# Linear attention and a routed mixture of experts on one core: a new order of the attention steps, 26 constant matmuls at the head of TensorE's queue, and one DMA for w_phi

## The chip, the cores and the metric

The kernel runs on one core of a Trainium2 chip. The metric is the device time of one execution in microseconds; several runs are summed up by their median. One execution was also profiled. In the profile PE is TensorE's matmuls and PEld its weight loads, DVE is VectorE, ACT is ScalarE, POOL is GpSimd, SP is SyncE; a "q" behind an engine's name means its sequencer, which issues DMAs and waits.

## What is computed

Two stages follow each other. The first is a linear attention (batch 8, 8 heads, 576 tokens, head size 64) with a feature map of 128 exponentials and their reciprocals; the second sends the 4608 tokens of 512 numbers through 8 experts of width 1024, whose results are mixed by a table P that eight rounds of row and column scaling make.

```python
def phi(x):
    proj = np.einsum('bhsd,df->bhsf', x, w_phi)
    proj = proj - np.max(np.abs(proj), axis=-1, keepdims=True)
    return np.concatenate([np.exp(proj), np.exp(-proj)], axis=-1)
q_p, k_p = (phi(q), phi(k))
kv = np.einsum('bhsf,bhsd->bhfd', k_p, v)
z = np.sum(k_p, axis=2)
num = np.einsum('bhsf,bhfd->bhsd', q_p, kv)
den = np.einsum('bhsf,bhf->bhs', q_p, z)[..., None] + 1e-06
# x = num / den, as (4608, 512)
...
P = np.exp(logits)                 # logits = x @ w_gate - max
for _ in range(8):
    P /= P.sum(1, keepdims=True) + 1e-09
    P /= P.sum(0, keepdims=True) + 1e-09
    P *= N / E
for e in range(E):
    out += P[:, e:e + 1] * (np.maximum(x @ w1[e], 0.0) @ w2[e])
```

## The kernel before

**How instructions get their order.** The kernel doesn't issue instructions directly. Each operation is handed to a `Plan` with its engine, an estimated duration, the keys that it reads and writes, and the buffers that it takes. `Plan.schedule` is a list scheduler that runs on the host when the kernel is built: again and again it starts the operation that can start soonest on its engine, and of several that can start at once, the one that was handed in first. What it puts out is the order of each engine's queue. On the chip each engine takes its queue strictly in that order and waits by semaphores, so an estimated duration changes no instruction, but it can change which one stands ahead. The helpers `pe(cols, ...)`, `act(el, ...)`, `dve(el, ...)` and `pool(el, ...)` take a size, from which the duration is worked out; `pe` counts cols/2400 us. `dma(queue, ...)` hands in a transfer with an assumed rate.

**Tiling of the attention.** For each of the 8 batches the first 512 tokens of 4 pairs of heads are worked on as pairs (32 in all), and the last 64 tokens of all heads together as the "rest". The work is cut into steps named by a letter; the string `order` has 322 letters, the n-th occurrence of a letter being that step's n-th piece. Its order is the order in which operations are handed in, and so their priority:

- `l`: loads half a batch of keys, queries and values (`load_qk`, `load_v`). For batches 0 and 1 keys and queries come in fp32 by SP's queue into `acc` tiles that are free then; for batches 2 to 7 in bf16 by POOL's queue into `qk`, and `t` transposes them by a DMA on SP's queue (`turn_qk`, line 550) into `qkT`. `e` loads the rests. A load waits for the maxima of the last `a` and `q` ahead of it.
- `a` (`pair_a`): for batches 0 and 1 first 8 fp32 transposes on TensorE (line 735) of a pair's keys and queries, cast to `qkT` by DVE (line 739) and ACT (line 743); then four token matmuls of the keys by `wphi2` (256 columns each, line 605), two reduces of the absolute maximum on DVE (line 597), four exponentials on ACT (line 601), and the products of the values by the exponentials of the maxima on POOL (line 793).
- `q`: the token matmuls of the queries, two reduces, one small exponential. `p`: two feature-row matmuls (512 columns) and four exponentials. `r` (`rest_a`): all of this for a batch's rest, with 4 fp32 transposes in batches 0 and 1 (line 661).
- `b`, `n`, `m`: the product of keys and values (line 875 copies it), and the two heads' outputs (matmuls of line 888, DVE lines 896 to 902). `c` turns the result into `xT`, on TensorE (line 917) or, in batches 3 to 6, by a DMA transpose. `g`: the rest's turn and the gate.
- `w` loads expert 0's weights. `u` and `d` are quarters of expert 0's first and second layer (`up0`, `down0`); an up step takes 8 matmuls of 512 columns, needs `c` of the batch's four pairs, and appears in the profile as `ps<-xT,w`. These steps fill TensorE's free time.

**Start of the program.** SP's queue issues the first pair's keys, queries and values; ACT's queue issues two DMAs that load the same `w_phi` (64 by 128, fp32) into the lower and the upper 64 partitions of `wphi_f`. DVE clears `wphi2` (a block diagonal of two copies of `w_phi`), casts each half into it (line 1027), clears the two `vrd` tiles (line 1036), and sets `colw`, a 128 by 128 tile of ones that the routing uses much later.

**After the attention.** `routing` makes P on DVE while TensorE works on expert 0, and experts 1 to 7 then run for some 780 us with a scheme of seven products instead of eight (lines 1391 and 1400). None of that is touched.

Of the kernel before, what the change touches and what calls it, by code (L numbers as in the profile page):

```python
# [13 lines left out]
ACT = mybir.ActivationFunctionType  # L14
# [322 lines left out]
def kernel(  # L337
# [11 lines left out]
    nc = tc.nc  # L349
# [26 lines left out]
    colw = const.tile([128, 128], BF16, name="colw")  # L376
# [11 lines left out]
    wphi_f = a_in.tile([128, DF], FP32, name="wphi_f")  # L388
# [3 lines left out]
    vrd = [a_in.tile([128, 2, NP, 2, D1], BF16, name=f"vrd{i}") for i in range(2)]  # L392
# [7 lines left out]
    def pe(cols, fn, r=(), w=(), takes=()):  # L400
        plan.op("PE", max(cols / 2400.0 + 0.0025, 0.031), 0.22, fn, r, w, takes)
# [4 lines left out]
    def dve(el, fn, r=(), w=(), shared=False):  # L406
        plan.op("DVE", el / 960.0 + 0.07, 0.15, fn, r, w, shared=shared)
# [7 lines left out]
    def dma(queue, nbytes, rate, fn, r=(), w=()):  # L415

        speed, unit = LINK.get(rate, (rate, 40))
        if nbytes == 2 << 20:
            speed, unit = 400, 150
        o = plan.op(queue, 0.8 if queue == "POOL" else 0.6, 0.0, fn, r, w, (), nbytes / speed)  # L420
        o.turn, o.unit = rate == 148, unit
# [67 lines left out]
    def new(tag):  # L489
        return R[tag].new()  # L490
# [113 lines left out]
    def mm(out_, lhsT, rhs, start, stop):  # L604
        nc.tensor.matmul(out_, lhsT=lhsT, rhs=rhs, start=start, stop=stop)  # L605
# [45 lines left out]
    def rest_a(b, t):  # L651

        r = {}
        bi = NP * (b - t["b0"])
        rT = new("rT")
        if b >= 2:
            rk = [(t["qk"], h, x) for h in range(2) for x in range(2)]
        if b < 2:
            ptr = new("PP")
            for pr in range(NP):  # L660
                pe(128, lambda pr=pr: nc.tensor.transpose(
                    ptr()[:, pr * 128:pr * 128 + 128],
                    acc[0][:, b, pr * 128:pr * 128 + 128], identf),
                    [("acc", 0, b, h, x) for h in range(2) for x in range(2)] + ["identf"],
                    [ptr, ("acc", 0, b)])
            dve(512, lambda: nc.vector.tensor_copy(
                out=rT().rearrange("p a b -> p (a b)"), in_=ptr()), [ptr], [rT])
        else:
            dma("SP", 1 << 17, 148, lambda: nc.sync.dma_start_transpose(
                out=rT(), in_=t["qk"]()[:, bi:bi + NP].rearrange("p a b c -> p (a b c)")),  # L670
                rk, [rT])
        m = new("m_r")
        r["E"] = [new(f"kr{x}") for x in range(2)]
        r["T"] = [new(f"qr{x}") for x in range(2)]
        r["r"] = new("r_r")
        r["em"] = new("em_r")
        own = r["E"] + r["T"] + [m, r["r"], r["em"]]
        pp = two(RM)
        tokens(pp, lambda c: rT()[:, c, :], NP, [rT], own)
        if TI:  # L680
            mk = [(m, x) for x in range(2)]
            for x in range(2):
                maxes(512, lambda x=x: m()[:, 2 * x], lambda x=x: pp[1][x]().rearrange(
                    "p (c f) -> p c f", c=NP), [pp[0][x * (1 - RM)]], [(m, x)])
            for x, s in ((0, 1.0), (1, -1.0)):
                exp(512, lambda x=x: r["E"][x]().rearrange("p a b -> p (a b)"),
                    lambda: pp[1][1](), s, pp[0][-1:], [(r["E"][x], 0)])
        else:
            mk = [(m, c) for c in range(2 - RM)]
            for c in range(2 - RM):  # L690
                n = NP // 2 * (1 + RM)

                def sc(c=c, n=n):
                    return pp[0][c]().rearrange("p (a b c) -> p a b c", a=n, b=2)

                maxes(256 * n, lambda c=c, n=n: m()[:, 0:3:2, n * c:n * c + n].rearrange(
                    "p b a -> p a b"), sc, [pp[0][c]], [(m, c)])
                for x, s in ((0, 1.0), (1, -1.0)):
                    exp(128 * n, lambda x=x, c=c, n=n: r["E"][x]()[:, n * c:n * c + n],
                        lambda sc=sc: sc()[:, :, 1, :], s, [pp[0][c]], [(r["E"][x], c)])  # L700
        r["Ek"] = [[(r["E"][x], c) for c in range(1 if TI else 2 - RM)] for x in range(2)]
        pt = new("P1")
        pe(512, lambda: mm(pt()[:, 0:512], wphi2[:, 0, :],
                           rT().rearrange("p a b -> p (a b)"), True, True),
           [rT, "wphi2"], [pt])
        for x, s in ((0, 1.0), (1, -1.0)):
            exp(512, lambda x=x: r["T"][x]().rearrange("p a b -> p (a b)"),
                lambda: pt()[:, 0:512], s, [pt], [r["T"][x]])
        exp(10, lambda: r["r"](), lambda: m()[:, 0], -2.0, mk, [r["r"]])
        pool(8, lambda: nc.gpsimd.tensor_scalar_mul(m()[:, 1], m()[:, 2], -1.0), mk, [(m, "neg")])  # L710
        em, vd = r["em"], vrd[b % 2]
        exp(10, lambda: em(), lambda: m()[:, 1:3], 1.0, mk + [(m, "neg")], [em])
        for h in range(2):
            rows = slice(h * 64, h * 64 + 64)
            pool(512, lambda rows=rows, h=h: nc.gpsimd.tensor_tensor(
                out=vd[rows, :, :, h, 0:D],
                in0=t["v"]()[rows, None, bi:bi + NP].to_broadcast([64, 2, NP, D]),
                in1=em()[rows, :, :, None].to_broadcast([64, 2, NP, D]), op=ALU.mult),
                [(t["v"], h), em], [("vrd", b % 2, h)])
            pool(80, lambda rows=rows, h=h: nc.gpsimd.tensor_copy(  # L720
                out=vd[rows, :, :, h, D], in_=em()[rows]),
                [em], [("vrd", b % 2, h, 1)])
        return r

    def pair_a(b, pr, t):
# [3 lines left out]
        if b < 2:  # L729
            g = t["f"]  # L730
            for x in (1, 0):
                ptr = new("PP")
                i = 2 * x + h0 // 2
                for c in range(4):
                    pe(128, lambda c=c, i=i, ptr=ptr: nc.tensor.transpose(  # L735
                        ptr()[:, c * 128:(c + 1) * 128], acc[g][:, i, c * 128:c * 128 + 128],
                        identf), [("acc", g, i), "identf"], [ptr])
                if x:
                    dve(512, lambda x=x, ptr=ptr: nc.vector.tensor_copy(
                        out=t["T"]()[:, x, 2 * h0:2 * h0 + 4, :].rearrange("p a b -> p (a b)"),  # L740
                        in_=ptr()), [ptr], [(t["T"], x, h0 // 2)])
                else:
                    act(512, lambda x=x, ptr=ptr: nc.scalar.copy(
                        out=t["T"]()[:, x, 2 * h0:2 * h0 + 4, :].rearrange("p a b -> p (a b)"),
                        in_=ptr()), [ptr], [(t["T"], x, h0 // 2)])
# [15 lines left out]
        def scores(x, pp):  # L761
# [32 lines left out]
            out=s["v"]()[:, :, :, 0:D],  # L794
# [219 lines left out]
    for b in range(2):  # L1014
        for i in range(2):
            halves[b, i] = new_half(b, i)
    load_qk(0, 0, 2, halves[0, 0])
    dma("ACT", 1 << 15, 100, lambda: nc.scalar.dma_start(out=wphi_f[0:64, :], in_=w_phi),
        w=["wphi_f0"])
    dma("ACT", 1 << 15, 100, lambda: nc.scalar.dma_start(out=wphi_f[64:128, :], in_=w_phi),  # L1020
        w=["wphi_f1"])
    load_v(0, 0, 2, halves[0, 0])
    pool(300, lambda: make_identity(nc, identf), w=["identf"])
    act(128, lambda: nc.scalar.copy(out=ident, in_=identf), ["identf"], ["ident"])
# [8 lines left out]
    load_qk(0, 4, 4, halves[0, 1])  # L1033
    load_v(0, 4, 4, halves[0, 1])
    for i in range(2):
        dve(450, lambda i=i: nc.vector.memset(vrd[i], 0.0),
            w=[("vrd", i, h, *y) for h in range(2) for y in ((), (1,))])
    dve(128, lambda: nc.vector.memset(colw, 1.0), w=["colw"])
    dma("SP", 1 << 14, 50, lambda: nc.sync.dma_start(
        out=wgate_f, in_=moe_w_gate.rearrange("(c p) e -> p c e", p=128)), w=["wgate_f"])  # L1040
    act(32, lambda: nc.scalar.copy(out=wgate, in_=wgate_f), ["wgate_f"], ["wgate"])
# [25 lines left out]
    def stage_r(b):  # L1067
        rs[b] = rest_a(b, rests[b])
# [4 lines left out]
    def stage_g(b):  # L1073
# [9 lines left out]
             "c": lambda j: pair_c(j // 4, j % 4, xbs[j]), "g": stage_g,  # L1083
             "u": lambda i: up0(i // 4, i % 4), "d": lambda i: down0(i // 4, i % 4)}
    order = (
        "lraeaepqbwlqaqawwabwmqlltnrbppnwqbppmrmanbqaqmwwacmpnpbccpwbtcnmqnaqbclupunm"
        "taumquglcapalbcpnqqdcenmucugbblnapmrcqdutabnqpmunpbambccddnqplanmqmducpblttb"
        "augnaqlnrbdcampcadmqeutunqcppmdcaqtdqabpbbmlrqtdnpmuaqualbnagnacctbmqulupran"
        "tdpmtdqcmdnpdabdancpcabbqmpumqbcdgnappqunburqcbugmmnqdcdanumupqbnucmcpnmbddp"
        "bqmpncncubncmmgccg"  # L1090
    )
    for i, n in enumerate(order):
        at[0] = i
# [626 lines left out]
        return {"out": stores, "X1": X1, "Y1": Y1, "Z1": Z1, "X2": X2, "X3": X3, "Z2": Z2, "X4": X4}  # L1720


    ORDER = "X1 x10 w10 x11 X2 x20 y10 x21 Z1 y11 X3 w11 x30 x31 x40 x41 w20 Y1 w21 X4 Z2".split()
    INNER = ("ib1 ia1 ib2 ib3 X1 ia2 ia3 ia5 ia6 ib5 x20 ib6 ia4 x30 ia7 x40 ib4 x21 X2 y10 "
        "ib7 Z1 x31 X3 w20 Z2 y11 w21 x41 Y1 X4").split()
    EARLY = ("w10 x10 X1 w11 y10 x11 x20 Z1 x30 w20 x21 X2 Y1 x31 w21 X3 Z2 X4 x41 y11 x40").split()
    END = "X1 p2 Y1 X2 Z1 p3 X3 Z2 X4 p0 p1".split()
    slots, wait = list(range(6)), []

    def take():  # L1730
# [91 lines left out]
```

## Time and profile before

| | |
|---|---|
| median of 3 runs | 1014.48 us (1013.58 to 1015.42) |
| profiled execution | 1013.5 us, of which the span from first to last instruction is 1011.7 us |
| TensorE busy | 996.5 us (99%), 8195 matmuls |
| VectorE, ScalarE, GpSimd busy | 851.8, 797.0 and 379.7 us |
| read from and written to memory | 92.62 MB and 14.55 MB |

The page first gives busy time by engine, then the span in 40 slices of about 25 us with a digit for the busy tenths, then DMA queues, the chain that ended last, and the costliest groups of instructions. Other views of the same trace give busy time for chosen stretches, instructions in order of time (with `[idle before <-releaser]`, what the engine had waited for), and DMAs with their time from issue to landing. Matmuls are pipelined: the time of one is longer than the distance to the next.

### The profile page before, as it was taken

Reading aid. Unit: us, or ns where it says so; the run is one execution under the profiler, and the core shown is the slowest. Engines: PE = TensorE matmul, PEld = TensorE weight load, DVE = VectorE, ACT = ScalarE, POOL = GpSimd, SP = SyncE. Lnnn points to the kernel's source line nnn. Section 1 sums busy time; section 2 is a strip of 40 time slices with the busy share of each in tenths; the row PEclk is TensorE's granted clock in tenths of the full one; section 3 lists DMA queues with packets and bytes.
Section 4 is the critical chain, followed back from the end, with each engine's and each line's share of the span. In section 5 each row is a group of like instructions: output and inputs, shape, how many; then the busy total and the mean of one; then the engine's idle time right before and its main releaser. Section 6 shows DMA issues by size and latency. Waiting matters only on the chain.

```text
span 1011.7 us, 22473 instructions
## 1 busy us (share of the span) xinstructions
PE 996.5 (99%) x8195; PEld 713.6 (71%) x8232; DVE 851.8 (84%) x1979; ACT 797.0 (79%) x1786; POOL 379.7 (38%) x418
## 2 busy tenths in 40 slices
PE   7899999999999999999999999999999999999998
PEld 5666666644566867787777777787778777787775
DVE  8999989986888988789788988898778978888775
ACT  8999999836888787777777777768776877777774
POOL 5778764400133323342333323332333333433333
PEclk9999999999999999999999999999999999999999
DMA  9999989150114411171116121341126111612443
GB/s 253 198 191 177 166 148 134 38 115 1 48 48 96 114 48 48 48 138 56 48 48 117 48 57 52 73 93 48 48 51 144 48 48 48 110 53 69 154 154 142
DMA packets 115087, 93.94 MB, mean 93 GB/s; under 512 B 54432, under 2 KB 97440, under 8 KB 114976
## 3 DMA queue, kind: packets, MB, share of 16 engines
q1 hardware_dynamic: 83024, 68.46, 26.4%
q0 software_dynamic: 31648, 23.86, 17.0%
q8 instruction: 64, 1.05, 0.5%
q14 instruction: 47, 0.39, 0.1%
q10 hardware_dynamic: 304, 0.20, 0.1%
HBM read 92.62 MB, written 14.55 MB: 106 GB/s over the span
## 4 chain that ended last, share of the span: by engine, by line
PE 93%; ACT 3%; DVE 1%; DMA 1%; issue 1%; DVEq 0%
PE ps L1391 42%; PE ps L1400 25%; PE ps L605 17%; PE ps L1487 7%; PE ps L888 2%; ACT k L601 1%; ACT q L601 1%; DMA xT<-wx 1%; DVE wx L597 0%; PE ps L735 0%; DMA acc<-in_k_dram 0%; ACT wx L601 0%; PE ps L917 0%; ACT kr L601 0%; DVE m L597 0%
## 5 line engine op out<-in xcount | busy, mean ns | idle before, releaser
L1671 POOL TENSOR_TENSOR acc<-acc,hx 128x512 f32<-128x512 f32 x186 | 236.0, 1269 | 555.0 <-ACT hx L1668 287.5
L1391 PEld LDWEIGHTS <-hs 128*128 128x128 bf16 x1984 | 194.1, 98 | 56.2 <-issue 0.4
L1462 DVE CUSTOM_DVE_ANT_0 hs<-ps,U 128x512 bf16<-128x512 f32 x252 | 167.0, 685 | 46.6 <-PE ps L1400 29.0
L1668 ACT ACTIVATE hx<-ps,P 128x256 f32<-128x256 f32 x372 | 161.2, 482 | 45.2 <-PE ps L1391 42.3
L1467 ACT ACTIVATE hs<-ps 128x512 bf16<-128x512 f32 x252 | 151.1, 609 | 52.6 <-PE ps L1400 45.8
L1656 DVE SCALAR_TENSOR_TENSOR acc<-ps,P,acc 128x256 f32<-128x256 f32 x372 | 163.2, 476 | 31.8 <-PE ps L1391 30.7
L1391 PEld LDWEIGHTS <-hx 128*128 128x128 bf16 x1488 | 145.5, 98 | 27.1 <-issue 0.6
L1459 ACT COPY ps<-ps 128x512 f32<-128x512 f32 x252 | 146.4, 597 | 12.5 <-PE ps L1487 6.0
L1391 PE MATMUL ps<-hx,hs 128*128 128x256 bf16 x992 | 142.4, 273 | 0.1
L1400 PE MATMUL ps<-X,T 128*128 128x512 bf16 x448 | 131.5, 379 | 0.1
L1499 DVE TENSOR_TENSOR ps<-ps,U 128x256 f32<-128x256 f32 x192 | 75.5, 426 | 36.1 <-PE ps L1487 27.0
L1400 PEld LDWEIGHTS <-T 128*128 128x128 bf16 x672 | 65.7, 98 | 47.1 <-issue 0.6
L1455 ACT COPY U<-ps 128x512 f32<-128x512 f32 x126 | 74.7, 593 | 14.2 <-PE ps L1487 12.8
L1391 PE MATMUL ps<-wx,hs 128*128 128x256 bf16 x560 | 81.5, 273 | 0.0
L1391 PE MATMUL ps<-wx,hx 128*128 128x256 bf16 x496 | 75.9, 273 | 0.0
L1391 PE MATMUL ps<-hx 128*128 128x256 bf16 x496 | 75.9, 273 | 0.0
L1400 PE MATMUL ps<-xT,T 128*128 128x512 bf16 x224 | 72.5, 379 | 0.0
L605 PE MATMUL ps<-xT,w 128*128 128x512 bf16 x271 | 70.1, 379 | 0.6
L605 PE MATMUL ps<-w,hx 128*128 128x512 bf16 x274 | 69.7, 379 | 0.5
L1391 PE MATMUL ps<-w,hx 128*128 128x256 bf16 x432 | 69.8, 273 | 0.0
L1391 PE MATMUL ps<-w,hs 128*128 128x256 bf16 x432 | 64.7, 273 | 0.0
L597 DVE TENSOR_REDUCE m<-ps 128x4 f32<-128x512 f32 x88 | 58.7, 679 | 3.2 <-ACT k L601 1.5
(168 smaller groups left out, 1934.4 us busy)
## 6 DMA issues: line engine op xcount, KB each, us to landing
X<-xd SPq DMA_DIRECT2D x72, 256.0 KB, 2.7
wx<-in_moe_w_dram POOLq DMA_DIRECT2D x8, 1024.0 KB, 12.4
v_m<-in_v_dram SPq DMA_DIRECT2D x15, 512.0 KB, 5.7
out_dram<-acc SPq DMA_DIRECT2D x14, 512.0 KB, 3.2
w<-in_moe_w_dram POOLq DMA_DIRECT2D x6, 1024.0 KB, 10.8
XI<-xd SPq DMA_DIRECT2D x24, 192.0 KB, 2.5
qk<-in_k_dram POOLq DMA_DIRECT2D x12, 256.0 KB, 5.7
qk<-in_q_dram POOLq DMA_DIRECT2D x12, 256.0 KB, 6.9
```

The source lines that it names most:

```text
L605: nc.tensor.matmul(out_, lhsT=lhsT, rhs=rhs, start=start, stop=stop)
L1391: pe(256, lambda i=i, k=k, z=z: nc.tensor.matmul(bank()[:, 256 * i:256 * i + 256], lhsT=lhs(k, i), rhs=rhs(k), start=first and z, stop=k = ...
L1400: pe(512, lambda k=k: nc.tensor.matmul(bank().rearrange("p (a b) -> p a b", a=2), lhsT=lhs(k), rhs=rhs(k), start=first and k == 0, stop=k ...
L1455: act(512, lambda: nc.scalar.copy(out=u[q]().rearrange("p a b -> p (a b)"), in_=w[q]()), bk(w[q]), [u[q]])
L1459: act(512, lambda: nc.scalar.copy(out=to[q](), in_=x[q]()), bk(x[q]), [to[q]])
L1462: dve(515, lambda: nc.vector._custom_dve(ADD_SAT, out=out_(q, i, j), in0=bank[q]().rearrange("p (a b) -> p a b", a=2), in1=u[q](), s0=3.0e ...
L1467: act(512, lambda: nc.scalar.activation(out=out_(q, i, j), in_=bank[q]().rearrange("p (a b) -> p a b", a=2), func=ACT.Relu, bias=0.0, scal ...
L1487: pe(256, lambda: nc.tensor.matmul(at(i, h)(), lhsT=blocks[lhs]()[:, fp], rhs=rhs(), start=start, stop=True, skip_group_check=True), [*xal ...
L1499: dve(256, lambda: nc.vector.tensor_tensor(out=at(i, h)(), in0=at(1, 0)(), in1=s(), op=ALU.add), [k[1, 0], (p5, n)], [k[i, h]])
L1656: dve(320, lambda n=n, ts=ts: nc.vector.scalar_tensor_tensor(out=acc[g][:, ts, 256 * j:256 * j + 256], in0=bank()[:, 256 * n:256 * n + 256 ...
L1668: act(370, lambda n=n: nc.scalar.activation(out=u()[:, n, :], in_=bank()[:, 256 * n:256 * n + 256], func=ACT.Copy, bias=0.0, scale=P[:, 4 ...
L1671: pool(695, lambda: nc.gpsimd.tensor_tensor(out=acc[g][:, 2 * i:2 * i + 2, 256 * j:256 * j + 256], in0=acc[g][:, 2 * i:2 * i + 2, 256 * j: ...
```

## The change

The fp32 transposes are handed to the planner as 256 columns instead of 128, and the two memsets of `vrd` as 990 elements instead of 450. The memset of `colw` moves to the head, and behind it come 26 matmuls of `colw` by itself (128 columns each) into a PSUM bank that nobody reads. `w_phi` is loaded by one DMA whose source names the 64 rows twice. `order` is another sequence of the same 322 letters. The last part of the diff, parentheses around two strings, changes nothing and is left out here.

```diff
@@ -658,7 +658,7 @@ rest_a
             for pr in range(NP):
-                pe(128, lambda pr=pr: nc.tensor.transpose(
+                pe(256, lambda pr=pr: nc.tensor.transpose(
                     ptr()[:, pr * 128:pr * 128 + 128],
                     acc[0][:, b, pr * 128:pr * 128 + 128], identf),
@@ -732,7 +732,7 @@ pair_a
                 for c in range(4):
-                    pe(128, lambda c=c, i=i, ptr=ptr: nc.tensor.transpose(
+                    pe(256, lambda c=c, i=i, ptr=ptr: nc.tensor.transpose(
                         ptr()[:, c * 128:(c + 1) * 128], acc[g][:, i, c * 128:c * 128 + 128],
                         identf), [("acc", g, i), "identf"], [ptr])
@@ -1015,10 +1015,13 @@
     load_qk(0, 0, 2, halves[0, 0])
-    dma("ACT", 1 << 15, 100, lambda: nc.scalar.dma_start(out=wphi_f[0:64, :], in_=w_phi),
-        w=["wphi_f0"])
-    dma("ACT", 1 << 15, 100, lambda: nc.scalar.dma_start(out=wphi_f[64:128, :], in_=w_phi),
-        w=["wphi_f1"])
+    dve(128, lambda: nc.vector.memset(colw, 1.0), w=["colw"])
+    warm = new("P1")
+    for i in range(26):
+        pe(128, lambda: mm(warm()[:, 0:128], colw, colw, True, True), ["colw"], [warm])
+    dma("ACT", 1 << 16, 100, lambda: nc.scalar.dma_start(
+        out=wphi_f, in_=bass.AP(w_phi.tensor, w_phi.offset, [[0, 2], *w_phi.ap])),
+        w=["wphi_f0", "wphi_f1"])
     load_v(0, 0, 2, halves[0, 0])
@@ -1033,9 +1036,8 @@
     for i in range(2):
-        dve(450, lambda i=i: nc.vector.memset(vrd[i], 0.0),
+        dve(990, lambda i=i: nc.vector.memset(vrd[i], 0.0),
             w=[("vrd", i, h, *y) for h in range(2) for y in ((), (1,))])
-    dve(128, lambda: nc.vector.memset(colw, 1.0), w=["colw"])
@@ -1083,11 +1085,11 @@
     order = (
-        "lraeaepqbwlqaqawwabwmqlltnrbppnwqbppmrmanbqaqmwwacmpnpbccpwbtcnmqnaqbclupunm"
-        "taumquglcapalbcpnqqdcenmucugbblnapmrcqdutabnqpmunpbambccddnqplanmqmducpblttb"
-        "augnaqlnrbdcampcadmqeutunqcppmdcaqtdqabpbbmlrqtdnpmuaqualbnagnacctbmqulupran"
-        "tdpmtdqcmdnpdabdancpcabbqmpumqbcdgnappqunburqcbugmmnqdcdanumupqbnucmcpnmbddp"
-        "bqmpncncubncmmgccg"
+        "rlaqeabwpnwelwawaqlbpqbqmweraqmtappnnabwacqlpntplmccamlqatbpqpcbrwwmtmlannql"
+        "pquqpbctutcbmlbneaanlmuaacabucrdmpumubqgqlbduaqnngqmcpqbbanpncmdqulcpdctgruq"
+        "ppamndcntbdabmpdaalnumqtbnnpcutbcumampdbdaaaqracuqmblpntqdnptumcqadbpucmcmnq"
+        "rbnndubqcpcbdpgbmdncgpqdpnmubnaqbumpmqcdmumqauadrcqppbndcmndcqbnuapbnqnuucbb"
+        "pgcpmdcnmmugmncccg"
     )
```

More of the change, by code (lines that the diff above doesn't have):

```diff
@@ L1720, in down7 @@
         return {"out": stores, "X1": X1, "Y1": Y1, "Z1": Z1, "X2": X2, "X3": X3, "Z2": Z2, "X4": X4}
-    ORDER = "X1 x10 w10 x11 X2 x20 y10 x21 Z1 y11 X3 w11 x30 x31 x40 x41 w20 Y1 w21 X4 Z2".split()
+    ORDER = ("X1 x10 w10 x11 X2 x20 y10 x21 Z1 y11 X3 w11 x30 x31 x40 x41 w20 Y1 w21 X4 Z2").split()
     INNER = ("ib1 ia1 ib2 ib3 X1 ia2 ia3 ia5 ia6 ib5 x20 ib6 ia4 x30 ia7 x40 ib4 x21 X2 y10 "
@@ L1726 @@
     EARLY = ("w10 x10 X1 w11 y10 x11 x20 Z1 x30 w20 x21 X2 Y1 x31 w21 X3 Z2 X4 x41 y11 x40").split()
-    END = "X1 p2 Y1 X2 Z1 p3 X3 Z2 X4 p0 p1".split()
+    END = ("X1 p2 Y1 X2 Z1 p3 X3 Z2 X4 p0 p1").split()
     slots, wait = list(range(6)), []
```

## The prediction

> **What bounds the kernel now.** I read the page's shares first, then the slices, then the table of stretches, then the order of time at the start, and last the groups and landings that a term needs.
>
> ```profile
> span 1011.7 us, 22473 instructions
> PE 996.5 (99%) x8195; PEld 713.6 (71%) x8232; DVE 851.8 (84%) x1979; ACT 797.0 (79%) x1786; POOL 379.7 (38%) x418
> ...
> PE   7899999999999999999999999999999999999998
> ```
>
> TensorE is busy for 99% of the span, and only the first two slices and the last are short. That average hides the start, so the stretches come next (columns: stretch, then busy us of PE, PEld, DVE, ACT, POOL, then granted clock, DMA share, GB/s).
>
> ```profile
> 4.00:10.00 6.00, 5.96 (x30) 4.28 (x30) 3.73 (x7) 3.54 (x8) 0.46 (x2) 1.00 0.97 243
> 10.00:25.00 15.00, 12.71 (x133) 8.67 (x132) 14.50 (x29) 14.84 (x40) 13.01 (x22) 1.00 1.25 284
> 25.00:45.00 20.00, 17.25 (x193) 12.05 (x193) 19.54 (x44) 19.93 (x53) 14.55 (x25) 1.00 1.31 201
> 125.00:200.00 75.00, 74.15 (x880) 48.97 (x893) 67.56 (x160) 71.26 (x173) 41.94 (x68) 1.00 0.69 112
> 400.00:1000.00 600.00, 599.94 (x4625) 452.30 (x4624) 496.80 (x1152) 459.14 (x1020) 198.08 (x161) 1.00 0.30 76
> ```
>
> From 400 us on TensorE never stops, and the change touches nothing there. From 10 to 45 us ACT and DVE are full (34.8 and 34.0 of 35 us) and TensorE is not. After the clock is up, a 256-column matmul follows the last one after about 0.11 us and a 512-column one after 0.22; by such spacings the matmuls of 25 to 45 us need about 13.0 of 20 us, so 7 us are free, 35%. Expert 0 is the filler for them, and its first up matmul (ps<-xT,w) stands at 44.67. Whatever is won must be won before 225 us: in the late start, in the ACT- and DVE-bound stretch to 45, and in the small holes after it. In the order of time the start looks like this:
>
> ```profile
> 3.87 2.08 PE L735 MATMUL ps<-identf,acc 128*128 128x128 f32 x8 [3.87 <-DMA acc<-in_k_dram]
> 4.06 0.22 DVE L1027 CAST wphi<-wphi_f 64x128 bf16<-64x128 f32 x1 [0.75 <-DMA wphi_f<-in_w_phi_dram]
> 4.99 0.69 DVE L739 CAST qkT<-ps 128x512 bf16<-128x512 f32 x1 [0.71 <-PE ps L735]
> 5.72 0.22 DVE L1027 CAST wphi<-wphi_f 64x128 bf16<-64x128 f32 x1
> 6.00 1.01 PE L605 MATMUL ps<-wphi,qkT 128*128 128x256 bf16 x4
> 6.80 1.06 PE L605 MATMUL ps<-qkT,wphi 128*128 128x512 bf16 x2
> 7.04 1.57 ACT L601 ACTIVATE k<-ps 128x512 bf16<-128x512 f32 x3 [0.47 <-PE ps L605]
> ...
> 15.78 0.60 PE L605 MATMUL ps<-wphi,qkT 128*128 128x256 bf16 x4
> ```
>
> The first exponentials, from which ACT runs without a pause, start at 7.04. Four token matmuls take 1.01 us at 6.00 and 0.60 at 15.78: TensorE runs at half pace at first, though the granted clock reads 1.00. The last slow matmul is near 8.7 us.
>
> **The change part by part.** The sum is made on the profiled execution, 1013.5 us with 1011.7 of span; the median of the runs is 1014.48, 1.0 above it, and I move every result to the median.
>
> *Warm-up.* 26 matmuls of 128 columns at half pace, some 0.107 us each (half of the 0.21 between slow 256-column ones), are 2.8 us. They wait only for colw's memset, 0.17 us, now first on DVE from 0.82, so they fill about 1.0 to 3.9, where TensorE had waited for the first keys until 3.87. That wait hides them; should they overrun, the first transposes wait 0.1 to 0.3 us. Their price is nothing. What they buy: the tokens take 0.41 less (1.01 to 0.60), the feature rows 0.43 (two at twice 0.21). The transposes at 3.87 probably stay slow. [...]
>
> *w_phi by one DMA.* It takes 0.61 us of issue off ACT's sequencer, hidden, since ACT waits for keys until 5.99. The landings are 3.2 and 3.7 us after issue now, so at 3.9 and 5.0; the second cast waits behind DVE's 4.99 to 5.68. Best case: one landing before 4.99, both casts before the qkT cast, tokens at 5.74 instead of 6.00, a gain of 0.26. Worst case: the transfer runs on few engines (rival 1). With the tokens' 0.41 and the feature rows' 0.43 the head is worth between -1.1 and +0.6. I take **-0.6**, nearest to the token row, 0.41, with part of the 0.26: ACT starts on the tokens, not on the feature rows.
>
> *Prices in the planner.* The 64 transposes of L735 and the 8 of L661 run at 0.118 us (16 in 2.04 less the last one's 0.27), and were planned at half of it; the vrd memsets took 0.93 us. No such edit costs anything by itself; they change which instruction comes first on each queue.
>
> *The new order.* It has the same 322 steps, so the same work; only its places change. The first up step needs c of the first four pairs, whose last inputs are step n of pair 3 in the old order (place 52) and step m of pair 3 in the new (place 53). Ahead of that point the new order has one a more, one q, one m, one b and one r fewer, two c more: on DVE (a reduce is 0.68, two to an a, q or r of batch 2; an m 1.1; a b 0.43; a c 0.33) 1.37 - 1.37 - 1.1 - 0.43 - 1.37 + 0.66 = -2.2 us. An up step started 2.2 us sooner fills 35% of that: -0.8. Beyond it the order can win at most what ACT idles from 45 to 200 us, 0.8 + 2.1 + 3.7 = 6.7 (30, 50 and 75 us less its busy time in the three stretches), and can lose as much. Nothing in the trace fixes the place between; I take a fifth, -1.4, since half of that idle time lies after 125 us, where DVE and TensorE have holes too. Order: **-2.2**, ends -6.7 and +5.3 (rival 2). It moves loads as well: on POOL each is an issue of 0.8 us ahead of the v products, and POOL's own idle time covers that after 45 us (22.3 busy of 30), less so before (14.6 of 20).
>
> **Sum.** -0.6 - 2.2 = -2.8, so 1010.7 for the profiled execution and **1011.7** as a median. After the start, the next thing late is ACT, which stays full until 45 us; so a shift of its first exponential reaches the end nearly whole.
>
> **Rival 1: w_phi lands later than now.** The source repeats w_phi by a leading step of zero, count 2. If that puts the transfer on two DMA engines, each has 64 rows of 512 bytes instead of 8. The queue's row:
>
> ```profile
> q10 hardware_dynamic: 160, 0.07, 1.3%
> ```
>
> is 1.3% of 16 engines for 20 us, 4.2 us for 160 packets, 26 ns each; 64 are 1.7 us alone, and twice that if SP's queue, full from 2.8 us on, takes every other turn. The first row moves at 2.8, so it lands at 5.0 to 6.7 with the 0.6 to 0.8 seen after the last row; with two casts of 0.22 the tokens start at 5.4 to 7.1. It also delays the keys on those two engines. Then the head is worth +0.6 at worst instead of -0.6: **1012.9**, no change that can be told. [...] No DMA of the trace has such a shape. [...] Against: the loss is capped by the tokens' 0.41, and DVE's casts wait for keys anyway. Chance as the deciding case 0.15.
>
> **Rival 2: batch 2's keys come late, slower than before.** Pair 8 is the first whose keys and queries come by a DMA transpose. Its a step moves from place 66 to 52, its load only from 22 to 18.
>
> ```profile
> 41.72 7.59 SPq L550 DMA_TRANSPOSE qkT<-qk  x2
> ...
> 51.20 1.29 PE L605 MATMUL ps<-wphi,qkT 128*128 128x256 bf16 x8 [0.28 <-DVE m L597]
> ```
>
> The first transpose is issued at 41.72, when the queries have landed, and lands 7.7 us later at 49.4; its first tokens run at 51.20, a margin of 1.7. In the new order two p and one r fewer stand ahead of that a: on ACT 2 x 4 x 0.52 (three exponentials take 1.57) + 2.9 (an r: 1.34 kr, 1.13 qr, 0.48 small ones) = 7.1 us. One a fewer stands ahead of the load: 2.9 (four exponentials, a cast of 0.58, a small one of 0.21). So the tokens are asked for 7.1 sooner, the data comes 2.9 sooner, and the shortfall is 7.1 - 2.9 - 1.7 = 2.5 us; if the full DMA engines (share 1.31) let nothing come sooner, 5.3. TensorE's queue is in order, so the p, n and m steps behind those tokens wait too, and ACT and DVE run dry where they are the bound. It decides once the landing is later than the tokens' turn. For it: the SP queue waits 31.2 us in all for queries to land ahead of these transposes. Against: a planner places that a when its data are expected. Without the order's gain and with a stall of 4: 1014.5 - 0.6 + 4 = **1017.9**. Chance 0.27.
>
> **Rival 3: nothing moves.** ACT and DVE are full from 10 to 45, so the order changes which work waits, and the earlier start is spent before a later landing. Head and order cancel within 1 us: **1014.2**. Chance 0.05.
>
> **How the numbers follow.** Forecast 0.53, rivals 0.15, 0.27 and 0.05. A difference under 0.2%, 2.0 us, is about what a measurement of this kernel can tell from none; so faster 0.53, same 0.20, slower 0.27. The low end, 1008.3, has the head at its best (-1.1) and the order at -5.1, short of its bound; the high end is rival 2's 1017.9. About one in ten is left out on each side.
>
> **What would show it.** Right: 26 short matmuls ahead of 3.9, four first tokens in 0.6 us, first exponentials near 6.4, first xT,w matmul near 42, ACT idle from 45 to 200 under 6. Wrong: w_phi landing after 5.7 (rival 1), TensorE or its weight loads idle for a qkT transpose between 40 and 60 us (rival 2), or ACT with pauses between 10 and 45, which would sink the forecast whatever the head does.

## The result, and the profile after

The changed kernel takes **1021.4 us** (median of 6 runs, 1020.5 to 1022.93) against 1014.66 for the kernel before (6 runs): a ratio of 1.0068 with a 95% interval of 1.0055 to 1.0081. It is slower by 6.7 us, where 1011.7 was forecast and 1017.9 was the upper end. The profiled execution took 1021.83 us, with 1020.0 of span, 8.3 more than the span before.

The page of the changed kernel, first shares and slices (here and below, line numbers are those of the kernel profiled; up to 1017 they are the same in both):

```profile
span 1020.0 us, 22509 instructions
PE 1000.0 (98%) x8218; PEld 716.7 (70%) x8258; DVE 852.4 (84%) x1979; ACT 797.2 (78%) x1786; POOL 379.7 (37%) x418
...
PE   7899899999999999999999999999999999999998
```

DVE, ACT and POOL do the same work as before to within 0.6 us. TensorE is busy 3.5 us longer, of which the 26 new matmuls are 2.96, and idle 20.0 us instead of 15.2. Counted without the new matmuls, which fill time that was empty anyway, the time in which TensorE does nothing of use has grown by 4.8 + 2.96 = 7.8 us. The stretches say where (columns as before: stretch, length, then busy us of PE, PEld, DVE, ACT, POOL, then granted clock, DMA share, GB/s):

```profile
4.00:10.00 6.00, 3.85 (x22) 2.77 (x22) 2.79 (x6) 2.51 (x5) 0.00 (x0) 0.88 0.73 193
10.00:25.00 15.00, 13.19 (x140) 9.93 (x140) 13.92 (x26) 14.26 (x39) 10.79 (x18) 0.93 1.10 278
25.00:45.00 20.00, 15.14 (x182) 10.62 (x180) 19.29 (x45) 19.93 (x52) 18.20 (x33) 1.00 1.64 210
75.00:125.00 50.00, 47.74 (x523) 30.97 (x530) 45.47 (x102) 44.02 (x103) 32.61 (x52) 1.00 1.24 193
125.00:200.00 75.00, 72.50 (x824) 47.71 (x838) 64.02 (x146) 70.79 (x176) 43.09 (x72) 0.98 0.60 106
400.00:1000.00 600.00, 599.93 (x4634) 453.14 (x4633) 498.16 (x1157) 461.57 (x1026) 198.32 (x161) 1.00 0.30 75
```

The kernel before had this from 75 to 125, the one of these stretches that the prediction doesn't show:

```profile
75.00:125.00 50.00, 49.58 (x556) 32.63 (x563) 46.69 (x106) 47.87 (x118) 39.31 (x62) 1.00 1.30 170
```

Set against before, TensorE loses 2.1 us from 4 to 10, 2.1 from 25 to 45, 1.8 from 75 to 125 and 1.7 from 125 to 200; from 10 to 25 it is busier, since more matmuls fall into this stretch (140 against 133) and its granted clock is only 0.93 there, so that many take longer (four token matmuls 0.82 us at 11.52, against 0.60 at 12.61). From 400 to 1000 us nothing differs. So the loss has a head and a later part. The head, in order of time:

```profile
1.04 2.96 PE L605 MATMUL ps<-colw 128*128 128x128 bf16 x26 [1.04 <-DVE colw L1018]
3.79 1.06 PE L735 MATMUL ps<-identf,acc 128*128 128x128 f32 x4
5.87 0.66 PE L735 MATMUL ps<-identf,acc 128*128 128x128 f32 x4 [1.01 <-DMA acc<-in_q_dram]
6.11 0.60 SPq L590 DMA_DIRECT2D v_r<-in_v_dram  x1
6.20 0.46 DVE L1030 CAST wphi<-wphi_f 64x128 bf16<-64x128 f32 x2 [2.89 <-DMA wphi_f<-in_w_phi_dram]
6.68 0.69 DVE L739 CAST qkT<-ps 128x512 bf16<-128x512 f32 x1
7.43 0.61 PE L605 MATMUL ps<-wphi,qkT 128*128 128x256 bf16 x4 [0.91 <-DVE qkT L739]
```

The new matmuls do what they are for: the queries' transposes take 0.66 us where the first four take 1.06, and the tokens 0.61 instead of 1.01. But `w_phi` lands at 6.2 instead of 5.0 and the first queries at 5.9 instead of 4.8. The first keys are not late (their transposes start at 3.79), but their cast (line 739) stands behind both casts of `w_phi` in DVE's queue, and DVE waits 2.89 us for that landing. So the tokens start at 7.43 instead of 6.00 and the first exponentials at 8.08 instead of 7.04. Two gaps of about 1 us in TensorE follow on each other, and the granted clock falls again (0.88 in this stretch, and 0.50 from about 8.5 to 12.0, where the matmuls are slow).

The later part is one event above all. The waits from 110 to 130 us (engine, line waited for: us in total, times, longest):

```profile
POOL qk L533 <- DMA qkT<-qk: 5.5, 1, 5.5
...
ACT em L601 <- POOL m L791: 3.3, 1, 3.3
```

and the chain of work from 112 to 126 us (start, us, what):

```profile
114.17 9.04 DMA qkT<-qk
...
123.78 0.56 POOL qk L533
124.33 0.27 issue
124.60 0.76 POOL qk L533
125.36 0.00 issue
125.37 0.48 POOL m L791 x2
125.85 0.02 issue
125.87 0.03 ACT em L601
```

A DMA transpose is issued at 114.17 and takes 9.0 us to land, where the planner had counted 5.8. GpSimd's next load of keys needs the `qk` buffer that this transpose reads, and its queue is in order: the negations of the maxima (line 791) behind the load wait 5.5 us, and ScalarE waits 3.3 for them. TensorE stops twice behind that, and its granted clock then falls to half (two of its instructions, and the stretch after them):

```profile
125.14 0.38 PE L605 MATMUL ps<-xT,w 128*128 128x512 bf16 x1 [1.29 <-DMA xT<-wx]
127.11 1.02 PE L605 MATMUL ps<-xT,w 128*128 128x512 bf16 x4 [1.60 <-ACT acc L1001]
...
128.10:131.40 3.30, 3.30 (x36) 2.50 (x34) 2.32 (x5) 2.79 (x10) 2.23 (x4) 0.50 0.50 68
```

The first of the two waits is for another DMA transpose, of `xT`. At 66.78 a transpose took 11.05 us and cost GpSimd 1.1, but the planner had counted 11.15 for it, and the kernel falls only about half a microsecond further behind its plan there. In the kernel before, the chain from 40 to 230 us holds one DMA only:

```profile
163.07 7.12 DMA xT<-wx
```

### The profile page after: what moved, and what is told of

It reads as the page before. It is cut to its first block, busy times and chain, and to the rows that moved or that the text cites. A ratio compares the mean times of both kernels' runs of the same rounds, so it can differ in the third digit from the quotient of the medians.

```text
span 1020.0 us, 22509 instructions
## 1 busy us (share of the span) xinstructions
PE 1000.0 (98%) x8218; PEld 716.7 (70%) x8258; DVE 852.4 (84%) x1979; ACT 797.2 (78%) x1786; POOL 379.7 (37%) x418
## 3 DMA queue, kind: packets, MB, share of 16 engines
q0 software_dynamic: 31648, 23.86, 16.7%
## 4 chain that ended last, share of the span: by engine, by line
PE 91%; ACT 3%; DMA 3%; POOL 1%; DVE 1%; issue 1%; SPq 0%; POOLq 0%; DVEq 0%; ACTq 0%
PE ps L1393 41%; PE ps L1402 25%; PE ps L605 15%; PE ps L1489 7%; DMA qkT<-qk 2%; PE ps L888 1%; ACT wx L601 1%; ACT k L601 1%; DMA acc<-in_k_dram 1%; ACT q L601 1%; PE ps L735 0%; POOL vrd L715 0%; POOL wx L793 0%; POOL qk L533 0%; DVE m L597 0%
```

## How far each kernel follows its plan

One more reading ties the runs together. The planner's own start time of each of the 1979 DVE instructions was set beside its start in the trace; the difference is the lag. Where the plan already holds a loss, the lag stays level; where the chip does something that the plan didn't foresee, it jumps. Lags in us, the largest jump between 50 and 140 us, and the end that the planner itself worked out (e1 to e9 are the experiments of the next section):

| kernel | lag at 15 us | at 52 | largest jump | at 360 | planned end |
|---|---|---|---|---|---|
| before | 0.9 | 1.4 | none | 1.8 | 1010.5 |
| after | 2.7 | 2.9 | 4.8, from 124 to 132 | 9.8 | 1010.9 |
| e1, after with two DMAs for w_phi | 0.5 | 0.4 | 4.3, from 92 to 99 | 8.2 | (as after) |
| e8, before with the new durations | 0.4 | 0.6 | none | 1.0 | 1016.5 |
| e2, before with the new order | 1.9 | 2.9 | 4.8, at 74 | 10.6 | 1019.2 |
| e9, e1 with half transposes | 1.1 | 2.0 | none | 3.6 | (as after) |

For the change: the plan is 0.4 longer, the head adds 2.7 - 0.9 = 1.8, and after 15 us the lag grows by 7.1 instead of 0.9, so 6.2 more. The sum, 8.4, is the 8.3 us of the spans. About 1 us of the jump in after, and of that in e1, comes behind the stop itself, while the granted clock is 0.50.

## The experiments

All are compared with the kernel before on the same chip. "Plan kept" means that each queue has the order of the kernel that the experiment starts from. The theories, by the letters that the expectations use for them: A blames the order, A1 the order through GpSimd's load that waits for its `qk` buffer, D the traffic of other DMAs, P a mismatch of order and durations, T single DMA transposes that land late, at whatever queue stands there.

**e1: w_phi by two DMAs again, plan of after kept.**

```diff
-    dma("ACT", 1 << 16, 100, lambda: nc.scalar.dma_start(out=wphi_f, in_=bass.AP(...)), ...)
+    dma("ACT", 1 << 16, 100, lambda: [nc.scalar.dma_start(
+        out=wphi_f[64 * i:64 * i + 64, :], in_=w_phi) for i in range(2)][1], ...)
```

> The changed kernel with the same planned order of every queue; only w_phi is loaded by two DMAs (one for each half of the partitions) in the place of the one. Theory A (most of the loss is in the new order, beyond 60 us; the head is a smaller part): w_phi lands near 5.0 instead of 6.2, the first exponentials start near 6.9 instead of 8.1, and the time is 1020.2, 1.2 below the changed kernel's 1021.4. Rival H (the late w_phi and the cold clock behind it are the loss): 1014.7, as before the change. If w_phi is not on the path at all: 1021.4.

Measured: 1020.12 us (1019.78 to 1023.21), ratio 1.0068 [1.0051, 1.0085]. That is 6.3 us above its kernel before, where the change is 6.7 above: a difference that these few runs don't tell from none. In the profile the head is mended: `w_phi` has landed by 4.85, the first exponentials start at 6.63, the first up step at 44.3 instead of 46.8. But a transpose issued at 85.54 now takes 9.59 us (planned 6.6), and this time TensorE stands at it. Its waits from 25 to 200 us, and the four token matmuls behind this one, which are slow (granted clock 0.50 from 95 to 98):

```profile
PE ps L605 <- DMA qkT<-qk: 3.2, 1, 3.2
...
95.17 1.04 PE L605 MATMUL ps<-wphi,qkT 128*128 128x256 bf16 x4 [3.21 <-DMA qkT<-qk]
```

So most of the loss has nothing to do with the head, and the stop moves to another queue when the head moves.

**e2 and e3: the orders exchanged.** e2 is the kernel before with nothing but the new `order` string, e3 the changed kernel with nothing but the old one.

> The kernel before with the new order of the steps alone: two DMAs for w_phi, no warm-up matmuls, the old planned durations. Theory A (the new order asks for loads whose buffers are not free yet): 1020 to 1021, some 6 above 1014.7. Rival H (the head is the loss): 1014.7. Rival P (the order is good only with the corrected durations, or the durations are what spoils the plan): 1012 to 1014.7 if the durations spoil it, over 1023 if the order needs them.

> The changed kernel with the old order of the steps: warm-up matmuls, one DMA for w_phi and corrected durations stay. Theory A: 1015 to 1016.5, the head's loss of 1 us with perhaps half a microsecond of a worse plan. Rival H: 1021. Rival P (the durations spoil the plan): 1018 or more.

Measured: e2 1030.61 us (1029.74 to 1031.17), ratio 1.0164 [1.0149, 1.0179]; e3 1021.35 (1019.04 to 1024.2), ratio 1.0075 [1.0053, 1.0096]. The old order with the other edits loses as much as the new one, so A alone falls. Each exchange is worse in the plan already (1019.2 and 1015.4), and each has its own late transpose besides: issued at 64.8 in e2 (8.2 us, planned 4.6), at 78.4 in e3 (8.7, planned 4.6), each followed by a jump of 4 to 5 us.

**e4: a third `qk` buffer, plan of after kept.** It takes away what GpSimd's load at 123 us had waited for.

```diff
+    R["qk"].make = make_qk   # slots 0 1 2 0 1 2 0 1 2 0 1 0; slot 2 lies in acc[4], free by then
```

> The changed kernel with the same planned order of every queue; the bf16 keys and queries of batches 2 to 7 go around three buffers instead of two (the third lies in the fp32 tile of token group 4, which is free at that time; the last three halves use the first two buffers only). So POOL's loads need not wait for a DMA transpose to land. Theory A1 (POOL's queue, standing at such a load, holds up the small products behind it, which ACT waits for): POOL's 6.6 us of waiting at line 533 go, the stop of ACT and PE near 123 us goes, and the time is 1016 to 1018. Rival D (the DMA engines or SP's queue of transposes are what is late, and the load only shows it): POOL's wait moves to another place and the time stays at 1020.5 to 1021.5.

Measured: 1025.15 us (1024.67 to 1027.6), ratio 1.0117 [1.01, 1.0134], slower still. GpSimd's wait is gone, and TensorE now stands for another transpose, in order of time:

```profile
129.87 2.29 PE L616 MATMUL ps<-xT,w 128*128 128x512 bf16 x5 [4.10 <-DMA xT<-wx]
```

An up step waits for an `xT` issued at 121.89, which takes 7.9 us (planned 4.1). A1 falls: the buffer was where the stop showed, not what made it.

**e5: no value loads for batches 3 to 7, whose steps use the values of batch 2 again; plan of after kept.**

```diff
-        dma("SP", nh << 17, 320, lambda: nc.sync.dma_start(
+        dma("SP", nh << 17, 320, lambda: None if b >= 3 else nc.sync.dma_start(
```

> The changed kernel with the same planned order of every queue, but without the ten loads of values for batches 3 to 7 (their steps use the values of batch 2 again): 5.2 MB less on the DMA engines between 60 and 180 us, everything else as it was. Theory D (keys' and xT's transposes land a few microseconds after the planned time because they share full DMA engines with the loads, and each such landing stops a queue that is in order): the transposes land sooner, the stops near 75 to 95 and at 123 us go, and the time is 1014.5 to 1016.5, that is 1021.4 less some 6, with the head's 1.3 to 1.8 left. Rival Q (what is late is the order on SP's or POOL's queue itself, not the traffic): 1020 to 1021.4.

Measured: 1023.13 us (1017.84 to 1025.69), ratio 1.0085 [1.0058, 1.0111]; the four runs lie 8 us apart. In the profiled one GpSimd's waits still hold a line of the same kind:

```profile
POOL qk L542 <- DMA qkT<-qk: 6.5, 3, 4.5
```

Less traffic doesn't bring the transposes in time. That speaks against D as far as the value loads go; loads of keys and queries weren't taken away.

**e6 and e7: the old plan kept, one head edit each.** e6 adds the memset of `colw` and the 26 matmuls ahead of all else; e7 loads `w_phi` by the single DMA.

```diff
+    self.head()   # e6 only: memset of colw, 26 matmuls of colw by itself into an unread bank
...
-    dma("ACT", ..., lambda: nc.scalar.dma_start(out=wphi_f[0:64, :], in_=w_phi), ...)      # e7 only
-    dma("ACT", ..., lambda: nc.scalar.dma_start(out=wphi_f[64:128, :], in_=w_phi), ...)
+    dma("ACT", ..., lambda: nc.scalar.dma_start(out=wphi_f, in_=bass.AP(...)), ...)
+    dma("ACT", ..., lambda: None, ...)
```

> The kernel before, planned exactly as before; ahead of all planned instructions stand colw's memset on DVE and 26 constant matmuls on TensorE. Theory W (they bring the clock up by about 5.3 us instead of 8.7, and the first tokens and feature rows run at full pace): first exponentials near 6.5 instead of 7.04, and the time 0.4 to 1.0 below the kernel before, 1013.0 to 1013.6. Rival N (the shift meets a later landing and is lost, or the clock falls again): 1013.9. Rival S (an earlier start shifts the whole plan against the landings and a queue stops): over 1015.

> The kernel before, planned exactly as before; only w_phi comes by the one DMA with the doubled source in the place of the two. Theory A: it runs on two DMA engines, lands near 6.2 instead of 5.0, delays the first queries by 1 us on those engines, and the first exponentials by 1 to 1.5; the time is 1015 to 1016. Rival: the delay is taken up by a later wait, 1013.9; or it shifts the plan against the landings and more is lost, over 1017.

Measured: e6 1013.50 us (11 runs, 1013.06 to 1015.11) against 1013.90 (21 runs), ratio 0.9997 [0.9988, 1.0006], no change; e7 1015.06 (11 runs, 1014.18 to 1015.47), ratio 1.0008 [0.9999, 1.0017], 1.2 us more by the medians, which the interval just doesn't tell from none. In e6, in order of time:

```profile
5.88 0.60 PE L606 MATMUL ps<-wphi,qkT 128*128 128x256 bf16 x4 [0.21 <-DVE wphi L1028]
...
6.52 1.59 ACT L602 ACTIVATE k<-ps 128x512 bf16<-128x512 f32 x3 [0.23 <-PE ps L606]
...
7.41 0.66 PE L736 MATMUL ps<-identf,acc 128*128 128x128 f32 x4 [0.48 <-DMA acc<-in_k_dram]
```

The exponentials start 0.52 us sooner than before, but the second pair's transposes then wait for its keys (7.41) and its queries, and the fp32 transposes of the first rest start at 10.20 against 10.22 before: the landings take the half microsecond back. In e7:

```profile
6.02 0.22 DVE L1027 CAST wphi<-wphi_f 64x128 bf16<-64x128 f32 x1 [2.72 <-DMA wphi_f<-in_w_phi_dram]
6.17 0.68 DVE L739 CAST qkT<-ps 128x512 bf16<-128x512 f32 x1
6.17 0.72 PEld L735 LDWEIGHTS ps<-identf,acc 128*128 128x128 f32 x4 [1.72 <-DMA acc<-in_q_dram]
6.17 1.12 PE L735 MATMUL ps<-identf,acc 128*128 128x128 f32 x4 [1.32 <-DMA acc<-in_q_dram]
```

One DMA of 64 KB lands about 5.3 us after its issue, and it holds up the queries, which land at 6.2 instead of 4.8.

**e8: the kernel before with nothing but the new durations (256 for 128 columns, 990 for 450 elements).**

> The kernel before with the corrected planned durations alone (fp32 transposes as 256 columns, the vrd memsets as 990 elements): old order of steps, no warm-up, two DMAs for w_phi. Theory P (the old order fits only the old durations; any change of a planned duration makes another plan, and it is this that costs): 1018 to 1021, near the changed kernel with the old order (1021.35) less the head's 1.3. Rival (prices alone are harmless and it is the head that made that one slow): 1014 to 1015.

Measured: 1019.38 us (1018.1 to 1022.33), ratio 1.0058 [1.0044, 1.0073]. Durations change nothing on the chip but the queues' order, and that order is 5.5 us worse. Here the plan says so itself (1016.5 instead of 1010.5) and the chip follows it with an even lag; TensorE's extra idle time stands from 45 to 75 us, where it is busy for 27.25 of 30 us against 29.26 before. P holds for this half: the old order was good with the durations that it stood beside.

**e9: e1 with transposes of half the size from batch 3 on: only the keys are turned, and the queries' half keeps what it held.**

```diff
+                nc.sync.dma_start_transpose(out=t["T"]()[:, 1],
+                    in_=t["qk"]()[:, 1].rearrange("p a b -> p (a b)"))   # for b >= 3
```

> The changed kernel with two DMAs for w_phi and the same planned order; the DMA transposes of batches 3 to 7 turn only the keys, half of the bytes, and the queries of those batches stay the old ones. Theory T (what is lost after 60 us is lost at one or two of these transposes that land 3 us or more after the planned time, and at queues in order that stand there): each lands earlier than planned, the stops at 95 and 127 us go, the instructions follow the plan to the end, and the time is 1013 to 1015, some 6 below the 1020.1 with full transposes. Rival Q (the transposes are not what is late, the plan's own order is bad on the chip): 1019 to 1020.

Measured: 1015.0 us (10 runs, 1014.13 to 1016.84), ratio 1.0008 [0.9997, 1.0019]: 0.8 above its kernel before, where e1 was 6.3 above. No instruction of TensorE, DVE, ACT or GpSimd was taken away or moved, and between 80 and 210 us as many token matmuls and loads of GpSimd wait on the transposes' semaphores as in e1 (9 and 7). What is less is the bytes, and with them the time for which SP itself is held by one transpose, 1.2 to 1.4 us against 1.7 to 4.9 in e1. Its stretches:

```profile
75.00:125.00 50.00, 48.98 (x536) 31.92 (x541) 45.84 (x103) 47.14 (x115) 36.81 (x59) 1.00 1.11 162
125.00:200.00 75.00, 74.15 (x870) 48.92 (x885) 68.23 (x162) 71.24 (x173) 39.73 (x65) 1.00 0.46 85
```

ACT does 47.1 us of work from 75 to 125, as in the kernel before (47.9), where after did 44.0, and TensorE has 74.15 of 75 us back in the last stretch. No transpose of half the size takes longer than 7.4 us, and the lag, which jumps by 4 to 6 us at one place in after, e1, e4 and e11, doesn't jump here. T holds. Whether the shorter transfer or SP's shorter part brings the landings in, this run doesn't tell apart.

**e10: e1 without the 26 matmuls, plan kept.**

> The changed kernel with two DMAs for w_phi and the same planned order, but the 26 constant matmuls are not issued. Theory W0 (the warm-up wins half a microsecond at the first exponentials, and the landing of the second pair's keys and queries takes it back): first exponentials near 7.1 instead of 6.6, all engines within 0.3 us of each other by 12 us, and the time is 1020 within 1. Rival W1 (the new plan needs the warm-up): the head's lag behind the plan grows by 1 us or more and the time is 1021 to 1022.

Measured: 1020.24 us (1018.97 to 1022.4), ratio 1.0062 [1.0047, 1.0078]. The exponentials start at 6.97 instead of 6.63 and the first rest's transposes 0.6 us later, yet the end can't be told from that of e1: the warm-up's gain doesn't show there.

**e11: e1 with the third `qk` buffer.**

> The changed kernel with two DMAs for w_phi and three buffers for the bf16 keys and queries (the third in the fp32 tile of token group 4; the last three halves use two). Theory T: POOL no longer stands at line 533, but its loads start earlier and share the DMA engines with the transposes of xT, which an up step of expert 0 waits for at the head of TensorE's queue; that stop takes the old one's place, 1019 to 1023. Rival A1 (POOL's stop is the cause): both stops go, 1013.5 to 1015.5.

Measured: 1023.63 us (1020.75 to 1024.99), ratio 1.009 [1.0071, 1.0108]. The stop is that of e4, an up step at 129.64 that waits 3.87 us for `xT`.

**e12: e1 with each transpose issued as two halves, keys first.**

> The changed kernel with two DMAs for w_phi and the same planned order; each DMA transpose of a half batch is issued as two, the keys' half first, then the queries' half, so that an a step waits for half of the bytes only. Nothing is left out. Theory T: keys land about as early as in the run that turned keys alone (1015.0), queries no later than before; POOL's loads still wait for both, so one of the two stops stays in part: 1015 to 1018. If a transpose's time is mostly a fixed cost and not its bytes: 1020 or more.

Measured: 1021.34 us (five runs: 1017.41, 1021.34, 1022.2, 1017.34, 1022.28), ratio 1.0066 [1.0045, 1.0087]; 1015 to 1018 was expected. In the profiled run, of 1017.41, transposes still stand in the chain, with 7.27 us from 59.84 and 6.55 from 113.08. Cutting the transfer in two with all its bytes still to move doesn't bring the end in reliably.

## Why the prediction was wrong, step by step

- **What bounds the kernel** held: the tail is untouched, and all 8.3 us are lost before 225 us.
- **Warm-up** was sized right and its fate wrong. The tokens gave 0.41 as forecast (0.60 in e6). "The transposes at 3.87 probably stay slow" was half right: the first four stay slow (1.06), the next four don't (0.66). In after and e6 the second four transposes are fast at 5.9 and 5.0, 4.8 and 4.0 us after the first of the 26 matmuls (1.04); in e1, with the same 26, all eight are slow still (1.99 us from 3.83). What sets the moment at which they turn fast, these runs don't show. But e6 gains 0.4 of 1013.9 by the medians, which its interval doesn't tell from none, since the next landing takes the shift back. The working said "a shift of ACT's first exponential reaches the end nearly whole"; that sentence failed.
- **w_phi by one DMA** went as rival 1 had it, and past its end. The queue's row of the first 20 us:

```profile
q10 hardware_dynamic: 130, 0.07, 1.1%
```

  30 packets fewer than 160: in both traces 128 of them are rows of 512 bytes, and 32 packets of 4 bytes became 2. In after the rows, nearly all of 27 ns, run in two trains from 3.3 us on, with 23 to 24 ns from row to row in a train and some 66 from 4.3 to 5.2 us, and the last starts at 5.49; in before up to 10 packets of the queue are under way at once, and its last row starts at 4.21. Two trains fit the two engines of the rival; no view names the engines. Its landing, 6.2, lies in the 5.0 to 6.7 of the rival; mis-sized was what it holds up. The rival had the tokens at 7.1 at the latest and capped the loss at 0.6, with "DVE's casts wait for keys anyway" against it. The keys were there, and their cast of 0.69 had to wait behind both casts of `w_phi`: 6.20 + 0.46 + 0.69 gives the tokens' 7.43 but for 0.1, and the exponentials came 1.04 late. (ACT, said to wait for keys until 5.99 before the change, waits there for the queries' transposes.) The queries came a microsecond late too, with SP's next issue (6.11 instead of 4.73, so all later loads), and the clock fell again. Alone it costs 1.2 us by the medians (e7, not told from none); in the change, the profiled spans of after and e1 differ by 1.4, their medians against their own kernels before by 0.5. The head as a whole, forecast at -0.6, is +1.8 in the lag.
- **Prices in the planner**, "no such edit costs anything by itself": true of the instructions, wrong as a term. With the old order they cost 5.5 us (e8).
- **The new order**, -2.2, is the step that failed, and with it the zero for the prices, since both act through one plan only. It was read from the DVE work that stands ahead of one step in the string, as though the string were the schedule. The first up step came at 46.8, and at 44.3 with the head mended, not near 42: the string is only a priority, and the planner itself sees no gain (1010.9 against 1010.5). In place of a gain the chip falls 6.2 us further behind the plan than before, 4.8 of it at one late transpose and the slow clock behind it. (The fifth taken for the part beyond 45 us is 1.3, not 1.4; that changes nothing.) ACT idles 10.5 us from 45 to 200 (30, 50 and 75 less 29.73, 44.02 and 70.79) where "under 6" was the sign of being right.
- **Loads on POOL**, "POOL's own idle time covers that after 45 us", counted the 0.8 us of issue and not the wait for the buffer ahead of it. That wait is the 5.5 us at 118 to 123.
- **Rival 2** had the mechanism, a transpose that lands late and an in-order queue that stands at it with other work behind, and the size (2.5 to 5.3). Place and queue were wrong: not the first transpose at 40 to 60, which cost TensorE no wait, but a later one from 114 to 123 us; in the change first GpSimd, with ACT and TensorE behind it. Its margin was also worked out from one landing, 7.7 us, taken as fixed. The `qkT` transposes between 60 and 200 us land in 5.8 us in the median before and 6.4 after, and the one that matters took 9.0.

Open is why single transposes land late. The planner, which shares the DMA rate between the transfers of SP's and of POOL's queue, foresaw some long ones, such as the 11 us at 66.78. The ones at which a queue stopped took 3.0 to 4.1 us more than it had counted: 9.0 for 5.8 in after, 9.6 for 6.6 in e1, 8.2 and 8.7 for 4.6 in e2 and e3, 7.9 for 4.1 in e4. The kernel before has such a one too: a `qkT` transpose issued at 113.7 takes 10.1 us, 2.6 over its plan, and nothing stands close enough behind it to stop. So it is the late landing together with a plan that has no room at that place. Half the bytes cure it, less traffic of values doesn't, and a split helps in some runs only. A plan that allows 3 to 4 us more for each transpose wasn't run, so that the new order could win with such slack stays untried; no version here beat the kernel before, and e6 equals it.

## What to carry to other kernels

A hand-made or searched order is worth what the durations behind it are worth: change an estimate or the order alone, and both must be found again (+5.5 and +16.7 us here), and a plan whose own end moves by 0.4 us can still lose 6 on the chip where it leaves no slack behind a transfer that scatters. When an order is judged, look at each in-order queue for the instruction that waits for a DMA, list what stands behind it, and compare the margin with the worst landing of that kind, not its median (11.05 against 6.5 us in after). An early gain in front of a stage that waits for landings can be given back at the next landing: in e6 0.52 us at the first exponentials were 0.02 at the first rest's transposes.

## What the runs showed of the hardware that was not expected

- A DMA transpose of the same `qk` tile takes from 4.3 to 11.05 us from issue to landing within one execution of after (4.3 to 10.1 before). At half the size it takes 3.0 to 7.4 in e9: between 60 and 200 us the median is 5.0 against 7.0 in e1, and the longest 7.4 against 9.6, so half the bytes save less than a third of the time.
- The 64 KB DMA whose rows ran in two trains landed about 5.5 us after issue in after, and the same DMA 5.3 in e7, against 3.2 and 3.7 for two of 32 KB before; a 256 KB load beside it landed 1.0 and 1.3 us later than before.
- TensorE's granted clock fell to 0.50 from about 8.6 to 12.0 us in after, behind two gaps of only 1.0 and 0.9 us; in e6, whose gaps there are under 0.6 us, it read 1.00 from 4 to 25 and matmuls stayed fast.
- The big stops of TensorE have a second price. In the profiles of after, e1, e3, e4 and e11 a stretch of some 3.5 us at a granted clock of 0.50 comes with them (3.4 in after, from 128.0 to 131.4; 7 us in e2), which adds about 1 us to the lag in after and e1. In before, e6, e7 and e8 the granted clock never falls between 4 and 1009 us (1.00 there in before, and a mean of 1.000 over the whole span in the other three). Not every stop does it: in e5 TensorE stood for 3.52 us at 116 and the clock stayed at 1.00.
